# The first stage of a one-core Fourier-mixing and SwiGLU kernel, re-ordered: loads, PSUM banks and weight products

## The chip, the cores and the metric

The kernel runs on one core of a Trainium2 chip. A core has a matrix engine (TensorE, PE in the profile), three engines for elementwise work (VectorE is DVE, ScalarE is ACT, GpSimd is POOL), and SyncE (SP), which here only issues DMAs. Each engine works through a queue of its own, in order; engines wait for each other by semaphores. ScalarE and GpSimd issue DMAs too, between their computing instructions. The metric is the time of one execution on the device in microseconds, as the median of several.

## The reference

```python
X = np.fft.fft(x, axis=1)          # x: 8 x 3008 x 256, float32
X = np.fft.fft(X, axis=2).real     # 8 x 3008 x 256
t = X.reshape(24064, 256)
g = t @ w_gate                     # 256 x 1536
v = t @ w_val                      # 256 x 1536
out = (g / (1 + exp(-g)) * v) @ w_out   # 1536 x 256
```

## The kernel before, in words

**Mixing.** Of each batch's 3008 rows the kernel computes the transform for 1504, as two parts P (even in the feature index) and Q (odd); sums and differences of the two give a row and its mirror. The feature transform is folded into the weights: `Wp` and `Wq` are the weights multiplied by a cosine and a sine table (`CD`, `SDt`), and `Wm` is `Wq` times -2, with which PSUM goes from a row to its mirror by accumulation.

**The row transform of batch 0** is the first stage (lines 257 to 664). The 3008 rows are four quarters of 752. Rows that share a cosine are added before any product: a row that counts up from a quarter's start (a "rise") and one that counts down from its end (a "fall"). 128 such pairs per quarter are the long set (tile `XA`: entries 0 to 3 are the rises, 4 to 7 the falls), 60 per quarter the short set (`XC0`, two quarters above each other in the partitions). Falls come from memory in groups of four rows in another order, so the rises are brought into the same order by a product with a permutation matrix (`place`, line 433, with `putA` or `putC`): its result lies in PSUM. `cross` or `cross_halves` (446, 449) adds the falls with the features turned round; `half_fold` (459) and `fold_d` (495) add or subtract the lower and the upper half of the features, which gives the even sums and the odd sums; `ends` (454) handles feature 0. `half_cast` (499) makes bfloat16 of them. Then `half_folded` (484, long set) and `folded_c` (490, short set) multiply the sums with cosine and sine tables (`Tab`) into two pairs of PSUM banks, `acc[0]` for the even and `acc[1]` for the odd sums; `row0` (619) adds row 0's contribution; `even_copy` (515) and `first_puts` (641) write the tiles `Pt` and `Qt`, the operands of the main stage. `first_w` (502) makes the first 512 columns of `Wp` and `Wq` from the raw weights that `load_w` (389) loads through GpSimd's queue, and `double` (511) makes `Wm` of them on GpSimd.

Everything in this stage stands in the order in which it is written, on each engine's queue. At its start SyncE issues all rises of the long set as one DMA (line 261), two falls, the rises of the short set (267) and its falls (270); ScalarE issues two falls of the long set (264); GpSimd issues the middle rows of the short set (404). TensorE meanwhile multiplies the all-zero matrix `sel` by itself 48 times (306). The tables' angles are computed on GpSimd (`turns`, 362) and VectorE (`angles`, 366), the sines on ScalarE. PSUM's eight banks are eight slots for the whole kernel: three named g, three v, two o; the first stage takes its banks from them.

**The main stage** (from line 666) runs over 24 tiles of up to 512 columns and 12 blocks of 128 hidden features each: products for gate and value (line 1015), silu on ScalarE, products on VectorE and GpSimd, and the output product with `w_out` (1279). The rest of the weights (products at 1501) and the transforms of batches 1 to 7 (1453) are put between. Its order on each engine is planned by a small scheduler in the kernel (`Sched`, from estimated durations and due times), and the plan starts from fixed offsets, so it does not depend on how long the first stage takes. The tiles of the main stage lie in the memory that the first stage's scratch (`tp`, `tq`) leaves.

The order around the change, after the tables:

```python
    psA = place(XA, putA, 4, ((psG, "g"), (psV, "v")))
    warm(8)
    for a in range(2):
        cross(FA[:, a], XA, psA, a)
```

Of the kernel before, what the change touches and what calls it, by code (L numbers as in the profile page):

```python
# [19 lines left out]
def kernel(  # L20
# [67 lines left out]
    Tab = const.tile([P, 2, 2, 2, NTAB], BF16, name="Tab")  # L88
    halfpi = const.tile([P, 1], F32, name="halfpi")
# [31 lines left out]

    def up_block(b, j, n):
        return rows_at(b, 2 * j - 1, [[2 * D, n], [R * D, 4], [1, 2 * D]])
# [121 lines left out]
    Ec0 = tp.tile([P, 2, 2, 1], F32, name="Ec0")  # L245
# [15 lines left out]
    q.dma_start(out=XA3[:, 0:4, :], in_=up_block(0, 1, P))  # L261
# [24 lines left out]
    nc.gpsimd.iota(putA, pattern=[[-LA, NA], [1, LA]], base=JA - 1, **iota)  # L286
# [6 lines left out]
    for a in range(2):  # L293
        fall_c(1, a, q)
        fall_c(0, a, q)
# [7 lines left out]
    for i in range(4):  # L303
        ps = psO.tile([P, T], F32, name="o")
        for j in range(12):
            nc.tensor.matmul(ps[:, 0:P], sel, sel, start=True, stop=True)
# [7 lines left out]
    mm_ = col("mm", 4)  # L314
# [28 lines left out]
    def turn_signs():  # L343
        n_ = col("n_", 4, I32)
# [10 lines left out]
    vts(putA, putA, scalar1=pcol, scalar2=None, op0=Alu.is_equal)  # L355
# [51 lines left out]
    nc.gpsimd.memset(sel[0:1, :], 1.0)  # L407
# [22 lines left out]
    weigh_ce()  # L430
    opposite(0)

    def place(X, put, n, pools):
        pss = []
        for a in range(n):
            pool, nm = pools[a % len(pools)]
            ps = pool.tile([P, 2, D], F32, name=nm)
            nc.tensor.matmul(ps.rearrange("p q d -> p (q d)"), put, X[:, a].rearrange("p q d -> p (q d)"),
                             start=True, stop=True)
            pss.append(ps)  # L440
        return pss

    def falling(X, pss, a):
        return (X[:, 7 - a] if len(pss) == 4 else X[:, 2 + a])[:, ::-1]

    def cross(to, X, pss, a):
        vtt(to[:, :, 1:D], pss[a][:, :, 1:D], falling(X, pss, a)[:, :, D - 1:0:-1], op=Alu.add)

    def cross_halves(to, X, pss, a):
        down = falling(X, pss, a)  # L450
        vtt(to, pss[a][:, :, 1:P + 1], down[:, :, D - 1:P - 1:-1], op=Alu.add)
        vtt(pss[a][:, :, P:D], pss[a][:, :, P:D], down[:, :, P:0:-1], op=Alu.add)

    def ends(to, X, pss, a):
        vtt(to, pss[a][:, :, 0:1], falling(X, pss, a)[:, :, 0:1], op=Alu.add)
# [3 lines left out]
    def half_fold(eo, to, low, pss, a):  # L459
        vtt(to, low[:, :, ::-1], pss[a][:, :, P:D], op=SUMS[eo])  # L460
# [8 lines left out]
    def warm(n):  # L469
        ps = psO.tile([P, T], F32, name="o")  # L470
        for i in range(n):
            nc.tensor.matmul(ps[:, 0:P], sel, sel, start=True, stop=True)

    def start_acc(eo):
        for q, (pool, nm) in enumerate(((psV, "v"), (psG, "g"))):
            acc[eo][q] = pool.tile([P, T], F32, name=nm)
# [7 lines left out]
    def half_folded(eo, a0, first):  # L484
        for q in range(2):
# [33 lines left out]

    psG.at = psV.at = 2  # L520
    psA = place(XA, putA, 4, ((psG, "g"), (psV, "v")))
    warm(8)
    for a in range(2):
        cross(FA[:, a], XA, psA, a)
    for a in range(2):
        ends(Eh[:, a], XA, psA, a)
    row_signs()
# [4 lines left out]
    for a in range(2, 4):  # L532
        cross_halves(FA[:, a, :, 1:P + 1], XA, psA, a)
    for a in range(2, 4):
        half_fold(0, EOA[0][1][:, a - 2], FA[:, a, :, 1:P + 1], psA, a)
    for a in range(2, 4):
        ends(Eh[:, a], XA, psA, a)
    start_acc(0)
    start_acc(1)
    psC = place(XC0, putC, 2, ((psO, "o"),))  # L540
    half_cast(0, 0)
    for a in range(2, 4):
        nc.scalar.copy(FA[:, a, :, P + 1:D], psA[a][:, :, P + 1:D])
    half_cast(0, 2)
    nc.scalar.activation(Z0.rearrange("p q k d -> p (q k d)"), zero.to_broadcast([P, 6 * P]), AF.Copy)
    opposite(1)
# [16 lines left out]
    for fn in early[5:]:  # L563
        fn()
    load_w(1, (0,))
    fold_d(1, 2)
# [3 lines left out]
    ptt(EOb[:, 1, 0:2], EOA[1][0], EOA[1][1], op=Alu.add)  # L570
    half_folded(0, 0, True)
# [9 lines left out]
    for a in range(2):  # L581
        half_fold(1, EB[:, 1, a], FC[:, a], psC, a)
# [78 lines left out]
    for c in copies[2:4]:  # L661
        c()
# [1102 lines left out]
```

## Time and profile before

| | us |
|---|---|
| median of 3 runs (lowest to highest) | 597.71 (597.52 to 597.75) |
| the profiled execution | 597.77 |
| its span, from the first instruction to the last | 596.0 |
| TensorE busy | 590.9 (99%) |
| VectorE, ScalarE, GpSimd busy | 568.6, 553.6, 533.5 (95%, 93%, 90%) |
| first product of the main stage starts | 18.20 |

A timeline row gives the start in us, the duration, the engine, the line of the kernel, the operation, the tiles (out<-in) with their shape, and how many instructions are merged in it; in brackets stands how long the engine was idle before it, and what released it. A row of a table of stretches gives for each engine the busy time and, in parentheses, the number of instructions, then the granted TensorE clock, the share of time in which the DMA engines were busy and the GB/s they moved. A queue row gives packets, MB, and share of the DMA engines. A row of waits gives who waited for whom, the total in us, how often, and the longest. In the DMA rows q1 is SyncE's queue, q10 ScalarE's, q0 GpSimd's. Busy TensorE time counts overlapping matmuls; TensorE is the engine that has no free time in this kernel.

### The profile page before, as it was taken

To read this page: it belongs to the slowest core of one execution; us is meant where nothing else is said; L and a number is where in the kernel's file an instruction comes from. 1 tells how busy PE (TensorE), PEld (TensorE's weight loads), DVE (VectorE), ACT (ScalarE), POOL (GpSimd) and SP (SyncE) were. 2 spreads that over 40 slices of the span, in tenths; PEclk is the share of its full clock that TensorE was granted. 3 is DMA by queue.
4 is the path that set the end of the run, shared out by engine and by line. 5 is a ranking of instruction groups with operands and counts; after the bars stand their busy time and mean duration, and the time that the engine had idled before them with its cause. 6 is when DMAs were issued, how large, how long until landed. Compare 5 with 4: busy or idle time off the path is not lost.

```text
span 596.0 us, 12394 instructions
## 1 busy us (share of the span) xinstructions
PE 590.9 (99%) x4014; PEld 390.6 (66%) x4014; DVE 568.6 (95%) x1062; ACT 553.6 (93%) x1071; POOL 533.5 (90%) x491
## 2 busy tenths in 40 slices
PE   9999999999999999999999999999999999999997
PEld 6456676666666666666666666666666666666686
DVE  9989999999999999999999999999999999999993
ACT  8768989999998899899999999999999999999995
POOL 9979999999999999999899998999889868687782
PEclk9999999999999999999999999999999999999999
DMA  9976772756244255285125122054121103202212
GB/s 251 161 222 229 185 235 71 194 165 222 82 149 126 73 139 137 68 273 159 54 82 168 37 64 63 19 152 143 46 63 37 47 19 88 67 28 63 60 54 81
DMA packets 61070, 68.17 MB, mean 114 GB/s; under 512 B 6744, under 2 KB 48668, under 8 KB 61006
## 3 DMA queue, kind: packets, MB, share of 16 engines
q1 hardware_dynamic: 57422, 64.44, 36.1%
q0 software_dynamic: 3216, 2.36, 2.9%
q8 instruction: 31, 0.51, 0.4%
q10 hardware_dynamic: 368, 0.59, 0.3%
q14 instruction: 33, 0.27, 0.2%
HBM read 40.21 MB, written 35.43 MB: 127 GB/s over the span
## 4 chain that ended last, share of the span: by engine, by line
PE 96%; DVE 0%; ACT 0%; issue 0%
PE o L1279 41%; PE g L1015 27%; PE v L1015 21%; PE g L1453 2%; PE o L1453 2%; PE v L1279 1%; PE o L1501 1%; PE g L622 0%; PE o L622 0%; PE g L1279 0%; PE o L1582 0%; PE g L1650 0%; DVE Wp L508 0%; ACT es L1289 0%; DVE Qt L646 0%
## 5 line engine op out<-in xcount | busy, mean ns | idle before, releaser
L1226 POOL TENSOR_TENSOR hm<-sv 128x1024 bf16<-128x1024 f32 (+2 forms) x137 | 254.7, 1862 | 32.3 <-ACT sv L1202 12.9
L1218 DVE SCALAR_TENSOR_TENSOR sv<-es,v 128x512 f32<-128x512 f32 (+2 forms) x262 | 174.0, 670 | 5.9 <-PE v L1015 4.3
L1279 PE MATMUL o<-Wo,hm 128*128 128x256 bf16 (+1 forms) x1128 | 163.7, 273 | 0.0
L1279 PE MATMUL o<-Wo,hp 128*128 128x256 bf16 (+1 forms) x1104 | 161.1, 272 | 0.0
L1229 DVE TENSOR_TENSOR hp<-sp,v 128x512 bf16<-128x512 f32 (+2 forms) x228 | 151.6, 671 | 1.9 <-PE v L1015 1.1
L1279 PEld LDWEIGHTS <-hm 128*128 128x128 bf16 (+2 forms) x1140 | 111.9, 98 | 58.0 <-issue 0.6
L1279 PEld LDWEIGHTS <-hp 128*128 128x128 bf16 (+2 forms) x1140 | 111.8, 98 | 55.3 <-issue 0.3
L1202 ACT ACTIVATE sv<-g 128x512 f32<-128x512 f32 (+2 forms) x181 | 119.0, 675 | 3.6 <-PE g L1015 3.1
L1127 ACT ACTIVATE sp<-g 128x512 f32<-128x512 f32 (+2 forms) x181 | 112.1, 621 | 5.9 <-PE g L1015 4.0
L1015 PE MATMUL g<-Pt,Wp 128*128 128x512 bf16 (+2 forms) x288 | 107.5, 374 | 0.0
L1015 PE MATMUL v<-Pt,Wp 128*128 128x512 bf16 (+2 forms) x288 | 106.2, 375 | 0.2 <-DVE Wp L508 0.2
L1015 PE MATMUL g<-Qt,Wq 128*128 128x512 bf16 (+2 forms) x288 | 105.4, 375 | 0.1
L1088 ACT ACTIVATE v<-bc,w 128x512 f32<-128x512 bf16 (+2 forms) x139 | 100.3, 726 | 1.9 <-DVE sv L1218 1.0
L1152 DVE SCALAR_TENSOR_TENSOR es<-bc,w,v 128x512 f32<-128x512 bf16 (+2 forms) x135 | 97.9, 732 | 2.1
L1150 ACT ACTIVATE es<-v 128x512 f32<-128x512 f32 (+2 forms) x139 | 86.0, 621 | 3.2 <-PE v L1015 1.6
L1015 PEld LDWEIGHTS <-Wp 128*128 128x128 bf16 x576 | 56.3, 98 | 26.0 <-DVE Wp L508 1.0
L1015 PE MATMUL g<-Qt,Wm 128*128 128x512 bf16 (+2 forms) x195 | 73.1, 376 | 0.0
L1131 DVE SCALAR_TENSOR_TENSOR sg<-bc,w,g 128x512 f32<-128x512 bf16 (+2 forms) x93 | 67.3, 724 | 1.6 <-PE g L1015 1.4
L1235 POOL TENSOR_TENSOR hp<-sp,pp 128x512 bf16<-128x512 f32 (+1 forms) x46 | 57.2, 1245 | 8.0 <-ACT pp L1232 7.8
L1202 ACT ACTIVATE sv<-sg 128x512 f32<-128x512 f32 (+2 forms) x93 | 63.6, 695 | 0.5 <-DVE sg L1195 0.5
L1195 DVE SCALAR_TENSOR_TENSOR sg<-sg,g 128x512 f32<-128x512 f32 (+2 forms) x93 | 61.6, 663 | 0.2
L1015 PEld LDWEIGHTS <-Wq 128*128 128x128 bf16 x437 | 42.7, 98 | 27.5 <-issue 0.4
(218 smaller groups left out, 788.7 us busy)
## 6 DMA issues: line engine op xcount, KB each, us to landing
out_dram<-ev SPq DMA_DIRECT2D x96, 128.0 KB
XA<-in_x_dram SPq DMA_DIRECT2D x30, 256.0 KB
tA<-in_x_dram SPq DMA_DIRECT2D x28, 256.0 KB
XA<-tA SPq DMA_DIRECT2D x14, 512.0 KB
XC<-in_x_dram SPq DMA_DIRECT2D x28, 120.0 KB
tC<-in_x_dram SPq DMA_DIRECT2D x28, 120.0 KB
XC<-tC SPq DMA_DIRECT2D x6, 480.0 KB
bc<-br SPq DMA_DIRECT2D x19, 128.0 KB
```

The source lines that it names most:

```text
L1015: nc.tensor.matmul(ps[:, :n], Wt[:, gv, fs], src[:, :n], start=start, stop=stop, skip_group_check=True)
L1088: nc.scalar.activation(T_[kv][:, :w], bc[t][:, :w], AF.Copy, scale=w0[:, 1, f:f + 1])
L1127: nc.scalar.activation(sp_to()[:, :w], T_[kg][:, :w], AF.Silu)
L1131: nc.vector.scalar_tensor_tensor(T_[keg][:, :w], bc[t][:, :w], w0[:, 0, f:f + 1], T_[kg][:, :w], op0=Alu.mult, op1=Alu.add)
L1150: nc.scalar.activation(T_[kes][:, :w], T_[kv][:, :w], AF.Copy, scale=2.0 if on_pool(u) > 1 else 1.0)
L1152: nc.vector.scalar_tensor_tensor(T_[kes][:, :w], bc[t][:, :w], w0[:, 1, f:f + 1], T_[kv][:, :w], op0=Alu.mult, op1=Alu.add)
L1195: nc.vector.scalar_tensor_tensor(T_[kgm][:, :w], T_[keg][:, :w], 2.0, T_[kg][:, :w], op0=Alu.mult, op1=Alu.subtract)
L1202: nc.scalar.activation(sv()[:, f % 2, w - 1::-1, 1], T_[kgm if by_dve else kg][:, :w], AF.Silu)
L1218: nc.vector.scalar_tensor_tensor(sv()[:, f % 2, w - 1::-1, 0], T_[kes][:, :w], 2.0, T_[kv][:, :w], op0=Alu.mult, op1=Alu.subtract)
L1226: nc.gpsimd.tensor_tensor(hts_(t)[1][:, f - 1:f + 1, :w], sv()[:, :, :w, 1], sv()[:, :, :w, 0], op=Alu.mult)
L1229: nc.vector.tensor_tensor(hts_(t)[0][:, f, :wp], T_[ksp][:, :wp], T_[kv][:, :wp], op=Alu.mult)
L1279: nc.tensor.matmul(st["ps"][:n, j, :], hts[t][minus][:, f, c:c + n], Wo[:, f, :], start=(f == 0), stop=(f == nF - 1))
```

## The change

Only the first stage is changed, and where PSUM banks come from in it.

- **Loads.** The rises of the long set are two DMAs of 512 KB (`rises_a(0)`, `rises_a(2)`) instead of one of 1 MB. ScalarE issues falls 3 and 2 (before: 3 and 1). SyncE issues rises 0 and 1, rises 2 and 3, fall 1, the short set's rises, fall 0 (before: rises, fall 2, fall 0, short set's rises). The middle rows of the short set are loaded by SyncE between the short set's falls, not by GpSimd.
- **Warm-up.** 33 products before the first placement instead of 48, and 5 after the second and 5 after the fourth placement instead of 8 after the fourth.
- **Banks.** The stage has PSUM pools of its own (`first_ctx`: one of two banks, six of one), closed at its end; then psG, psV and psO are made. The third and fourth set lie side by side in the pool of two banks, so `half_fold` and `ends` take both in one instruction.
- **Order on VectorE.** The comparison for `putA` goes to GpSimd (with its iota, between the two pairs of turns). The crossing of the fourth set comes after the ends of the first two. The turn signs come ahead of the first `first_puts`. All four weight copies come between `first_puts` of the even and of the odd sums.
- **Order on TensorE.** The first gate weights (`first_w(0, ...)`) come right after the first half of the even sums, the value weights (`first_w(1, ...)`) before the odd sums; row 0 is done for one half of the odd sums at a time, and the copy of that half (`even_copy(1)`) stands between.
- **Order on ScalarE.** `opposite(0)` before `weigh_ce`, `opposite(1)` before the clearing of `Z0`.
- **Order on GpSimd.** `fold_d(1, 2)` and the sum into `EOb` come before the load of the second gate weights (`load_w(1, (0,))`), the heads after it; the row signs and the setting of `sel`'s first row come at the end of the stage, ahead of `double`.
- **Scratch.** `mm`, `Ec0` and `n_` lie in a new constant tile `mEc` and in `turn_sign`, not in scratch.

```diff
-    psG = Slots("psG", 3, space=bass.MemoryType.PSUM)
-    psV = Slots("psV", 3, space=bass.MemoryType.PSUM)
-    psO = Slots("psO", 2, space=bass.MemoryType.PSUM)
+    first_ctx = ExitStack()
+    banks = [first_ctx.enter_context(tc.tile_pool(name=f"bank{i}", bufs=1, space=bass.MemoryType.PSUM)) for i in range(7)]
...
+    def rises_a(a):
+        q.dma_start(out=XA3[:, a:a + 2, :], in_=rows_at(0, R * a + 1, [[2 * D, P], [R * D, 2], [1, 2 * D]]))
...
+    rises_a(0)
     nc.scalar.activation(w0[:, 0, 0:1], zero, AF.Silu)
     fall_a(3, nc.scalar)
-    fall_a(2, q)
-    fall_a(1, nc.scalar)
+    rises_a(2)
+    fall_a(2, nc.scalar)
+    fall_a(1, q)
+    rises_c(q)
     fall_a(0, q)
-    rises_c(q)
...
+    fall_c(1, 0, q)
+    q.dma_start(out=XC0[NCR:64 + NCR + 1:64, 2:4, 0], in_=rows_at(0, 0, [[2 * R * D, 2], [R * D, 2], [1, D]]))
+    fall_c(0, 0, q)
+    for hi in (1, 0):
+        fall_c(hi, 1, q)
...
+    warm(33)
...
     turns(ti[0], kf, 0)
+    nc.gpsimd.iota(putA, pattern=[[-LA, NA], [1, LA]], base=JA - 1, **iota)
+    pts(putA, putA, scalar1=pcol, scalar2=1.0, op0=Alu.is_equal, op1=Alu.mult)
     turns(ti[1], kf, 1)
     more_iotas()
-    nc.gpsimd.dma_start(out=XC0[NCR:64 + NCR + 1:64, 2:4, 0],
-                        in_=rows_at(0, 0, [[2 * R * D, 2], [R * D, 2], [1, D]]))
...
-    psA = place(XA, putA, 4, ((psG, "g"), (psV, "v")))
-    warm(8)
...
-    row_signs()
+    place(b0, XA, putA, 0)
+    place(b1, XA, putA, 1)
+    warm(5)
+    place(b23[:, 0], XA, putA, 2)
+    place(b23[:, 1], XA, putA, 3)
+    warm(5)
+    for a, ps in enumerate((ps0, ps1)):
+        cross(FA[:, a], ps, down01[:, a])
     load_w(0, (0,))
     fold_d(0, 0)
     load_w(0, (1,))
     fold_d(1, 0)
...
+    cross_halves(FA[:, 2, :, 1:P + 1], ps23[:, 0], down23[:, 0])
+    for a, ps in enumerate((ps0, ps1)):
+        ends(Eh[:, a], ps, down01[:, a])
+    cross_halves(FA[:, 3, :, 1:P + 1], ps23[:, 1], down23[:, 1])
+    half_fold(0, EOA[0][1], FA[:, 2:4, :, 1:P + 1], ps23)
+    ends(Eh[:, 2:4], ps23, down23)
...
+    fold_d(1, 2)
+    ptt(EOb[:, 1, 0:2], EOA[1][0], EOA[1][1], op=Alu.add)
     load_w(1, (0,))
-    fold_d(1, 2)
+    half_folded(0, 0, True)
...
+    turn_signs()
     hd = tp.tile([P, 2, 2, 1], F32, name="hd")
...
-    half_folded(0, 0, True)
+    first_ws = two_banks(0)
+    copies = [first_w(0, k, 1, first_ws[:, k]) for k in range(2)]
     half_folded(0, 2, False)
...
     od0 = even_copy(0)
...
+    copies += [first_w(1, k, k, one_bank(3 + k)) for k in range(2)]
+    start_acc(1, 5, 6)
     for a in range(2):
         folded_c(1, a, True)
-    half_folded(1, 0, False)
...
     nc.gpsimd.iota(kfO, pattern=[[4, GH]], base=1, **iota)
+    row_signs()
+    nc.gpsimd.memset(sel[0:1, :], 1.0)
...
     first_puts(0, od0, (0, 1))
+    for c in copies:
+        c()
     for i in range(2):
+        half_folded(1, 0, False, (i,))
         row0(0, i, acc[1][i])
-    copies[0]()
-    copies[1]()
-    turn_signs()
-    od1 = even_copy(1)
-    copies += [first_w(1, k, k, psO.tile([P, T], F32, name="o")) for k in range(2)]
-    first_puts(1, od1, (0,))
-    for c in copies[2:4]:
-        c()
-    first_puts(1, od1, (1,))
+        if i == 0:
+            od1 = even_copy(1)
+    first_puts(1, od1, (0, 1))
     tmp_ctx.close()
+    first_ctx.close()
+
+    psG = Slots("psG", 3, space=bass.MemoryType.PSUM)
```

More of the change, by code (lines that the diff above doesn't have):

```diff
@@ L301, in more_iotas, with warm @@
             nc.gpsimd.iota(putC[:, pm - NCR:pm], pattern=[[-2 * LC, NC_], [2, LC]], base=2 * (NCR - LC) + hi, **iota)
[L303 to L306, printed above, removed]
+    def warm(n):
+        for i in range(n):
+            nc.tensor.matmul(idle[:, 0, 0:P], sel, sel, start=True, stop=True)
+    warm(33)
     small = {}
@@ L467, with start_acc, of_sets @@
     acc = [[None, None], [None, None]]
[L469 to L476, printed above, removed]
+    def start_acc(eo, *at):
+        acc[eo] = [one_bank(i) for i in at]
+    def of_sets(bank):
+        return bank.rearrange("p a (q d) -> p a q d", q=2) if len(bank.shape) == 3 else bank.rearrange("p (q d) -> p q d", q=2)
     def set_cols(ps, tab, a):
```

111 lines of the change are left out of this document (48 added, 63 removed).

## The prediction

> **What bounds the kernel now.** I read the page first, then who waited for whom on TensorE, then the instructions of the first 24 us in order of time, engine by engine, then the DMA of the same stretch.
>
> ```profile
> span 596.0 us, 12394 instructions
> ```
>
> ```profile
> PE v L1015 <- DVE Wp L508: 0.2, 1, 0.2
> ```
>
> Beside its start, this is the only wait of TensorE (PE) in the run: after 19.5 us it never stands still, and the order on each engine in the main stage is the same in both kernels. So what the first stage gains or loses on TensorE by about 22 us is what the kernel gains or loses.
>
> ```profile
> 1.04 5.30 PE L306 MATMUL o<-sel 128*128 128x128 bf16 x48 [1.04 <-DVE sel L258]
> 6.13 1.36 PE L438 MATMUL g<-XA,putA 128*128 128x512 f32 x2
> ...
> 9.91 0.61 PE L472 MATMUL o<-sel 128*128 128x128 bf16 x8
> 10.36 1.94 PE L438 MATMUL o<-XC,putC 128*128 128x512 f32 x4
> 12.13 0.48 PE L488 MATMUL v<-Tab,EOb 128*128 128x377 bf16 x2
> ...
> 18.20 0.57 PE L1015 MATMUL g<-Pt,Wp 128*128 128x480 bf16 x2
> 18.90 0.36 PE L1015 MATMUL g<-Qt,Wq 128*128 128x480 bf16 x1
> 19.50 0.38 PE L1015 MATMUL v<-Pt,Wp 128*128 128x480 bf16 x1 [0.24 <-DVE Wp L508]
> ```
>
> TensorE runs on without a gap: 48 warm-up products to 6.13, four placements of the long set, 8 warm-ups, two placements of the short set, and from 12.13 to 18.20 (6.07 us) the sums, the first weights and row 0. Then it is held up at 18.90 by the odd tile and at 19.50 by a weight copy. The change touches just these: the warm-up count, the load before the first placement, the weight copy.
>
> **The change part by part.**
>
> *Rises in halves, 33 warm-ups.* In the stretches from 0, GB/s (the last column) times time is what the DMA has moved; below stand the queues up to 5.5 us, and SP's last two loads of the first stage:
>
> ```profile
> 0.00:4.00 4.00, 2.96 (x28) 2.97 (x29) 3.12 (x27) 3.24 (x6) 3.22 (x13) 1.00 0.46 136
> 0.00:9.00 9.00, 7.96 (x54) 6.50 (x55) 8.05 (x37) 7.92 (x13) 7.90 (x23) 1.00 0.79 279
> ```
>
> ```profile
> q1 hardware_dynamic: 524, 1.05, 58.5%
> q10 hardware_dynamic: 38, 0.08, 3.6%
> ```
>
> ```profile
> 5.97 1.81 SPq L270 DMA_DIRECT2D XC<-in_x_dram  x2
> ```
>
> The rises (1.05 MB) were through by 5.5 us, and the SP load that waits for their landing went out at 5.97: landing is 0.47 us behind the last byte. A half is 0.52 MB; 136 GB/s x 4.0 us = 0.54 MB, so the first half lands at about 4.0 + 0.47 = 4.5. The warm-ups cost (6.13 - 1.04) / 48 = 106 ns each; 33 end at 4.55. The first placement starts at 4.6 instead of 6.13.
>
> The eight later warm-ups took (10.36 - 9.91) / 8 = 56 ns, half as much: the clock doubled in between, and the first placement (1.36 us, against half of the short set's 1.94) shows that it did so around 6.1 to 7.5. Starting at 4.6, the first placement (at full speed (12.13 - 10.36) / 2 = 0.88) therefore costs 0.88 x 106 / 56 = 1.67, the second about 1.0, the other two 0.88 each, with 0.28 for 5 warm-ups ahead of them and behind: 9.6. The short set's rises now queue behind 1.05 MB and three falls of 0.26: through at 2.36 MB, 8.5 us by 279 GB/s, landed by 9.2 even if 0.2 late. Their placements run from 9.6 to 11.4, not 10.36 to 12.13. TensorE has gained 0.75 us there.
>
> *The last fall now queues behind the short set's rises*, at the mark of 2.62 MB instead of 2.10. 279 x 9 = 2.51 MB, so 9.4 at that rate, landed at 9.85 at the earliest; some 0.8 later, 10.6, if the first weight load (0.26 MB), which is issued 0.9 us earlier than before, goes through the engines ahead of it. I take 10.1, nearer the early end, as that load is issued after it. Who needs the fall is the crossing of the fourth set:
>
> ```profile
> 10.11 0.43 DVE L451 TENSOR_TENSOR FA<-v,XA 128x256 f32<-128x256 f32 x1
> ...
> 11.71 0.41 DVE L451 TENSOR_TENSOR FC<-o,XC 128x256 f32<-128x256 f32 x1
> ```
>
> ```profile
> 12.08 0.38 ACT L543 COPY FA<-v 128x254 f32<-128x254 f32 x1
> ```
>
> The crossing ran at 10.11. VectorE (DVE), relieved of the comparison for putA, comes to it about 0.4 us earlier and then stands until 10.1. Two sets folded at a time is the same elements in two instructions fewer (together below 0.15 us). So VectorE reaches the short set at 11.7 (11.71), and ScalarE (ACT) ends its copies of the upper halves at 12.08 + 0.38 = 12.46, as before. The gain of the placements stops here.
>
> *Weights ahead of the odd sums.* VectorE's end of the stage was:
>
> ```profile
> 15.73 1.20 DVE L646 TENSOR_TENSOR Pt<-g,od 128x188 bf16<-128x188 f32 x5 [0.64 <-ACT od L517]
> ...
> 18.07 0.77 DVE L646 TENSOR_TENSOR Qt<-g,od 128x188 bf16<-128x188 f32 x3
> 18.77 0.68 DVE L508 CAST Wp<-o 128x512 bf16<-128x512 f32 x1
> ```
>
> TensorE begins the sums at 11.4. After the first four products (0.65) come the first weights, into the two banks that ScalarE's copies free at 12.46: a wait of 0.5. So the main stage starts at 11.4 + 6.07 + 0.5 = 18.0 (18.20). VectorE fills its 0.64 us of idle time with the turn signs, moved ahead, and takes the weight copy in front of the odd tile: 18.07 - 0.64 + 0.68 = 18.11, no change for the odd tile, and 18.90 stays. But the value product of 19.50 then follows at once, at 19.15: 0.35 us gained.
>
> *What is pushed behind on GpSimd (POOL)*, which issues DMAs and computes in one queue:
>
> ```profile
> 7.25 0.19 POOL L407 MEMSET sel<- 1x128 bf16 x1
> 7.53 0.47 POOL L357 TENSOR_SCALAR sgo<-pc 128x1 f32<-128x1 f32 x1
> 8.12 0.26 POOL L358 TENSOR_SCALAR sgo<-sgo,sgn 128x1 f32<-128x1 f32 x1
> 8.32 0.82 POOL L394 DMA_DIRECT2D W<-in_moe_w_gate_dram  x1
> ...
> 12.03 0.73 POOL L394 DMA_DIRECT2D XA<-in_moe_w_gate_dram  x1
> 12.78 1.10 POOL L497 TENSOR_TENSOR Fc<-FA 128x512 f32<-128x512 f32 x1
> ...
> 18.89 1.35 POOL L512 TENSOR_SCALAR Wm<-Wq,m 128x512 bf16<-128x512 bf16 x2
> ```
>
> ```profile
> 21.79 0.37 PE L1015 MATMUL v<-Qt,Wm 128*128 128x480 bf16 x1
> ```
>
> The odd fold (12.78) needs ScalarE's copies and starts at 12.46 + 0.1 = 12.57. From it to the doubling of the mirrored weights Wm (18.89) were 6.11 us. Into this stretch come the weight load from ahead of the fold (12.78 - 12.03 = 0.75), the row signs (8.32 - 7.53 = 0.79) and sel's memset (0.19): 1.73. The doubling starts at 12.57 + 6.11 + 1.73 = 20.41 and its second half ends 1.35 later, at 21.76. TensorE used that half at 21.79 and, 0.35 us earlier, would want it at 21.44. It gets it at 21.9, a semaphore's 0.1 later: the 0.35 us are lost in this wait, and 0.1 with them. POOL then is 1.5 us late on work that TensorE asks for much later.
>
> *The middle rows' DMA from POOL to SP; putA's iota and comparison between POOL's two pairs of turns.* POOL drops an issue and gains a comparison, and has putC by 7.5, wanted at 9.6. SP has one issue more among its short loads; they ended at 5.97 + 1.81 = 7.78, and their data stand behind 2.6 MB anyway. Nothing.
>
> *opposite(1) ahead of clearing Z0* on ScalarE: Z0 is ready one copy later, below 1 us; SP's next loads wait for it, and for those the first fold of batch 1:
>
> ```profile
> 39.17 2.35 POOL L181 TENSOR_TENSOR SDf<-XC 128x1020 f32<-128x1020 f32 x1 [1.95 <-DVE hp L1053]
> ```
>
> POOL stood 1.95 us before that fold with nothing else due: no cost; without that cover, up to 1 us on POOL. Scratch moved: no instruction.
>
> **Sum.** +0.1 us. The profiled execution took 597.77 us (the span of 596.0 and 1.8 around it), 0.06 above the median of 597.71. Forecast 597.8; of its own 597.5 to 598.4, as the last fall lands from 9.85 (-0.25) to 10.6 (+0.5).
>
> **The rivals.**
>
> *The gain stays.* If POOL is at the doubling 0.4 us earlier than I add up, TensorE keeps its 0.35: 597.4. For it: the fall may land early, and two rows of one form on POOL differ by up to 0.1 us. Against it: 1.73 us of moved work. More than 0.2% (1.2 us, about what can be told from no change here) would need the doubling at 19.1, which the rows exclude.
>
> *The clock does not rise in time (slower).* Before, TensorE was busy without a break from 1.04 until the clock rose. Now it may stand between 4.55 and the first half's landing. If that keeps half speed through all four placements they end at 4.6 + 4 x 1.67 + 0.5 = 11.8, and the fourth set is crossed at 11.8 instead of 10.1, +1.7; if the clock rises during the third, +1.1. The chains of VectorE and POOL shift by it: 598.9 to 599.5. [...]
> The Trainium skill, "TensorE: Matmul & The Clock Gate", Part 1 (the HAM clock gate), says that the clock is released after a busy window of about 3.4 us which runs free of the kernel's start; the 106 and 56 ns above agree with its cold and warm spacing. By that rule any gap before the release is a risk.
> The Trainium skill, "DMA: Bandwidth & Descriptors", Queues, rings and completion order, says that an engine serves its queues in turn, packet by packet. By it the fall on ScalarE's queue would mix with the first half, which would land about 0.65 us later and open such a gap. The queue rows speak against it: by 5.5 us queue 10, ScalarE's, had moved 0.08 MB.
>
> *A weight load comes late (slower).* The load of 12.03 is now issued behind the odd fold and sum, at 12.57 + 1.10 + 1.26 = 14.9. The sum's row, the landing of the four weight loads into XA, and the first product with one of them:
>
> ```profile
> 14.42 1.26 POOL L570 TENSOR_TENSOR EOb<-Fc 128x512 bf16<-128x512 f32 x1
> ```
>
> ```profile
> DMA to landing us min/median/max: 5.0/5.5/7.8
> ```
>
> ```profile
> 20.52 0.59 PE L1501 MATMUL o<-XA,CD 128*128 128x512 bf16 x2
> ```
>
> At 5.5 us to landing it is there at 20.4; that product stood at 20.52 and is wanted at 20.2, a wait inside the one above. At the longest landing of these loads, 7.8, it is 22.7 and TensorE loses 2.2 against before: 599.9. It decides from 5.7 us on. Against it: the load of 12.03 landed in a queue of first-stage loads that is gone by 15.
>
> *The halves do nothing.* If the first half lands no earlier than the whole did (5.97), placements start at 6.0, the short set's at 10.0, and all limits behind stay: 597.8 again, with the clock's risk.
>
> **How the numbers follow.** POOL's wait, +0.1: 0.52. The gain stays: 0.18. Halves do nothing, same time: 0.06. Clock: 0.12. Late weight load, or another loss of its size in the main stage: 0.10. Far faster by something unseen: 0.02. Faster by over 0.2%: 0.05, with part of the second case; within: 0.77; slower: 0.18, part of the clock's lying at the edge. The range of 8 in 10 takes in the first two cases and the lower half of the clock's: 597.1 to 599.1.
>
> **What would show it.** First placement at 4.6 and longer than 1.36; the short set's at 9.6; the fourth set crossed at 10.1 after a wait of VectorE for a DMA; main stage begun at 18.0, its first value product right behind the odd tile at 19.15; the doubling at 20.4, and a wait of TensorE for Wm from POOL of about 0.4 us near 21.5, the only new one. Wrong if the doubling starts by 20.0, if placements after the second take over 1.2 us, or if TensorE waits for a weight load.

## The result, and the profile after

The changed kernel takes 599.62 us (median of 7 runs, 598.79 to 600.42) against 597.71 (7 runs, 597.40 to 597.92): a ratio of 1.0032, 95% interval 1.0020 to 1.0043. It is slower by 1.9 us, where no change was forecast (597.8, with 8 chances in 10 between 597.1 and 599.1). Its runs also lie further apart: 1.6 us from lowest to highest, 0.5 before. (That 0.5 is of seven runs. Of the 121 runs of the kernel before that were made beside all the experiments, 11 lie above 598.5, up to 599.66; no profile shows why.) The profiled run has the lowest time of the seven (598.79, span 597.0), so it shows only a part of the loss, 1.0 us of span.

The waits of TensorE in the changed kernel behind its start (who waited for whom, total, how often, longest):

```profile
PE b L505 <- ACT FA L549: 0.7, 1, 0.7
PE o L1513 <- DMA XA<-in_moe_w_gate_dram: 0.5, 1, 0.5
PE g L1027 <- DVE Qt L656: 0.4, 1, 0.4
PE b L493 <- DVE EOf L463: 0.3, 1, 0.3
```

None of them is the one forecast, for `Wm`. The first and the third were in the sum; the fourth was not; the second is the rival of the late weight load. In order of time, on TensorE:

```profile
4.85 2.24 PE L445 MATMUL b<-XA,putA 128*128 128x512 f32 x4
...
9.59 1.96 PE L445 MATMUL b<-XC,putC 128*128 128x512 f32 x4
11.39 0.81 PE L488 MATMUL b<-Tab,EOb 128*128 128x377 bf16 x4
12.85 0.59 PE L505 MATMUL b<-W,CD 128*128 128x512 bf16 x2 [0.66 <-ACT FA L549]
...
18.68 0.58 PE L1027 MATMUL g<-Pt,Wp 128*128 128x480 bf16 x2
19.70 0.36 PE L1027 MATMUL g<-Qt,Wq 128*128 128x480 bf16 x1 [0.44 <-DVE Qt L656]
...
21.58 0.60 PE L1513 MATMUL o<-XA,CD 128*128 128x512 bf16 x2 [0.51 <-DMA XA<-in_moe_w_gate_dram]
...
22.86 0.37 PE L1027 MATMUL v<-Qt,Wm 128*128 128x480 bf16 x1
```

The first half of the stage gains what was forecast: the sums begin at 11.39, not 12.13. By the main stage it is gone (18.68 against 18.20), and at the product that stood at 21.79 the kernel is 1.07 us late. On VectorE and on GpSimd:

```profile
10.37 0.43 DVE L452 TENSOR_TENSOR FA<-b,XA 128x256 f32<-128x256 f32 x1
...
11.98 0.41 DVE L452 TENSOR_TENSOR FC<-b,XC 128x256 f32<-128x256 f32 x1
...
13.76 0.42 DVE L452 TENSOR_TENSOR FC<-b,XC 128x256 f32<-128x256 f32 x1 [0.44 <-DMA XC<-in_x_dram]
...
18.86 1.20 DVE L656 TENSOR_TENSOR Qt<-b,od 128x188 bf16<-128x188 f32 x5 [0.70 <-PE b L638]
```

```profile
12.88 1.09 POOL L497 TENSOR_TENSOR Fc<-FA 128x512 f32<-128x512 f32 x1 [0.95 <-DVE b L453]
14.04 1.27 POOL L572 TENSOR_TENSOR EOb<-Fc 128x512 bf16<-128x512 f32 x1
15.25 0.74 POOL L407 DMA_DIRECT2D XA<-in_moe_w_gate_dram  x1
...
20.72 1.36 POOL L512 TENSOR_SCALAR Wm<-Wq,m 128x512 bf16<-128x512 bf16 x2
```

The four weight loads into `XA`, from issue to landing:

```profile
DMA to landing us min/median/max: 6.2/6.8/9.2
```

(5.0/5.5/7.8 before). The gate load goes out 3.2 us later than before (15.25 against 12.03), and these loads now take 1.2 to 1.4 us longer. The gate load itself took 5.0 us before and 6.3 now, so that it lands 4.5 us later (21.5 against 17.1).

### The profile page after: what moved, and what is told of

Its sections match the earlier page's. It is cut to its first block, busy times and chain, and to the rows that moved or that the text cites. A ratio compares the mean times of both kernels' runs of the same rounds, so it can differ in the third digit from the quotient of the medians.

```text
span 597.0 us, 12369 instructions
## 1 busy us (share of the span) xinstructions
PE 590.4 (99%) x4001; PEld 388.9 (65%) x4001; DVE 568.6 (95%) x1059; ACT 553.4 (93%) x1071; POOL 534.3 (89%) x491
## 4 chain that ended last, share of the span: by engine, by line
PE 97%; DMA 1%; POOL 1%; DVE 1%; issue 0%; ACT 0%; DVEq 0%; POOLq 0%
PE o L1291 41%; PE g L1027 27%; PE v L1027 21%; PE g L1465 2%; PE o L1465 2%; DMA XA<-in_moe_w_gate_dram 1%; PE b L445 1%; PE v L1291 1%; PE o L1513 1%; PE o L632 0%; PE g L632 0%; PE g L1291 0%; DVE b L453 0%; POOL EOb L572 0%; POOL t L377 0%
```

## The experiments

Times are given as the ratio of the means to the kernel before, run beside it on the same chip, with the 95% interval; 0.001 is 0.6 us. The changed kernel stands at 1.0032. The first load of gate weights into `XA` is called the gate load; the second sequence is batch 1, the loads of which SyncE issues behind those of the first stage.

### One order or one transfer undone

**gate_load_early**: the second chunk of the gate weights is loaded where it was loaded before.

```diff
+    load_w(1, (0,))
     fold_d(1, 2)
     ptt(EOb[:, 1, 0:2], EOA[1][0], EOA[1][1], op=Alu.add)
-    load_w(1, (0,))
```

> The changed kernel, but the second chunk of the gate weights is issued where it was before the change: ahead of the odd fold on POOL, not behind it and the sum EOb. Theory 1 (the late gate load is the loss): the issue goes from 15.25 to about 12 us, the data land at 17 to 18, the wait of 0.51 us of PE in L1513 for the gate weights goes, and the median falls by 0.5 us or more below the changed kernel's 599.6, with a smaller scatter. Theory 2 (the short set's falls arrive late, so the even and odd folds of the short set and the tiles Pt and Qt come late): the wait is only exchanged for another one, PE's first tile starts at 18.7 as in the changed kernel, and the median falls by less than 0.2. Theory 3 (the moved row signs and the memset hold up the doubled weights): nothing changes that is beyond 0.2.

Measured: 1.0018 (1.0009 to 1.0028), 598.13 to 599.98. The load goes out at 11.84, the wait for it is gone, and in this kernel's timeline the product of 22.86 stands at

```profile
21.88 0.37 PE L1027 MATMUL v<-Qt,Wm 128*128 128x480 bf16 x1
...
23.66 0.60 PE L1513 MATMUL o<-XA,CD 128*128 128x512 bf16 x2 [0.40 <-ACT sg L1083]
```

that is 0.09 behind the kernel before, as the sum of the prediction had it; another 0.40 comes right behind. By the ratios some 0.8 us of the 1.9 go. The scatter stays (1.9 us): this is not the whole cause. (The two intervals overlap; the run before_gate_late below settles the mechanism.)

**middle_on_pool**: the middle rows' load goes back to GpSimd. **both_back**: both edits.

```diff
     fall_c(1, 0, q)
-    q.dma_start(out=XC0[NCR:64 + NCR + 1:64, 2:4, 0], in_=rows_at(0, 0, [[2 * R * D, 2], [R * D, 2], [1, D]]))
     fall_c(0, 0, q)
...
     more_iotas()
+    nc.gpsimd.dma_start(out=XC0[NCR:64 + NCR + 1:64, 2:4, 0], in_=rows_at(0, 0, [[2 * R * D, 2], [R * D, 2], [1, D]]))
```

> The changed kernel, but the middle rows of the short set are issued by POOL behind its last tables, as before the change, so that SP has one issue less between its short falls. Theory 2 (SP's issue stands behind a semaphore of an earlier load, so that the last two short falls land at 12.97 and 13.63 in place of 11.69 and 12.19): the short set's second fold on DVE no longer waits 0.44 us for its data, Qt comes 0.4 to 0.7 earlier, and the median falls by 0.4 to 0.7 us below the changed kernel. Theory 1 (late gate load): the first tiles come earlier, but PE then waits that much longer for the gate weights, and the median falls by less than 0.2.

> The changed kernel with both: the gate load ahead of the odd fold and the middle rows on POOL. If theories 1 and 2 each hold a part, the gains add up: 1.0 us or more below the changed kernel in the profile, near the kernel before. If only one of them is the cause, this run equals the better of the two single ones within 0.2.

Measured: 1.0036 (1.0024 to 1.0048) and 1.0017 (1.0008 to 1.0026). The wait of VectorE for the short set's falls is not there, and in middle_on_pool the main stage starts at 18.44; the time does not fall. (Two further profiles of the changed kernel itself, below, lack that wait too, so the edit need not have removed it.) Both edits together are no better than the gate load alone. Theory 2, the late falls of the short set, falls as a cause of the loss. The profile of middle_on_pool (span 598.8) shows something else, a wait of TensorE in the main stage, near 62 us, taken up below.

**rises_whole**: the rises are one DMA again.

```diff
-        q.dma_start(out=XA3[:, a:a + 2, :], in_=rows_at(0, R * a + 1, [[2 * D, P], [R * D, 2], [1, 2 * D]]))
+        q.dma_start(out=XA3[:, a:a + 4, :], in_=rows_at(0, R * a + 1, [[2 * D, P], [R * D, 4], [1, 2 * D]]))
...
-    rises_a(2)
```

> The changed kernel, but the long set's rises are one DMA again, first on SP, and the falls keep the changed order and queues. The prediction's step 1 says that this costs the 0.75 us by which the short set is placed earlier, and nothing at the end, because the last fall sets the fourth crossing: within 0.2 of the changed kernel. Theory 2 says that one DMA less on the hardware queues shifts which load each later issue waits for: the last two short falls leave earlier, and the median falls by 0.3 to 0.7. Theory 4 (what scatters is the time of the clock's release, which hangs on when PE begins its unbroken work): a later first placement changes the scatter of the runs, not the waits.

Measured: 1.0066 (1.0050 to 1.0082), 600.16 to 603.26. Within the stage the forecast holds: TensorE waits 1.61 us for the rises, and the main stage starts at 18.84, only 0.16 later than with halves. But the wait for the gate weights grows to 0.72 (the load goes out at 15.92), and a wait of 0.68 for ScalarE follows at 29.6. So the halves are worth 2 us here by the ratios, and most of what the profile shows of it lies behind the stage; what the longer runs add to it no profile shows. Theory 4, that the clock's rise makes the scatter, finds no support: in the three profiles of the changed kernel the first two placements take 2.24, 2.51 and 1.98 us, as the clock rises later or earlier in them, but the sums begin at 11.39, 11.38 and 11.16, 0.23 us apart, and the spans lie 2.1 apart.

**zeros_early**: ScalarE clears `Z0` before its copies of `FA`. **zeros_and_gate_early**: this and the gate load.

```diff
     half_cast(0, 0)
+    nc.scalar.activation(Z0.rearrange("p q k d -> p (q k d)"), zero.to_broadcast([P, 6 * P]), AF.Copy)
     for a in range(2, 4):
         nc.scalar.copy(FA[:, a, :, P + 1:D], ps23[:, a - 2, :, P + 1:D])
     half_cast(0, 2)
     opposite(1)
-    nc.scalar.activation(Z0.rearrange("p q k d -> p (q k d)"), zero.to_broadcast([P, 6 * P]), AF.Copy)
```

> The changed kernel, but ACT writes the zeros Z0 before the copies of FA, in the 1.27 us in which it waits, and not after the opposite tables. SP's first zero fill of XC, which waits for Z0, then leaves at 12 to 13 us in place of 14.80 (13.74 in the kernel before), and every load of the second sequence behind it on SP with it. Theory 5 (the second sequence's loads are late: POOL's fold of XC at 40.3 instead of 39.2, and when it comes much after 40.3, as at 41.54 and 41.93 in two runs above, POOL's products come late and ACT and PE wait for them): the fold of XC begins before 39.5, and the median falls from 599.6 to 598.6 to 599.0, with a scatter of under 1 us; the profile's waits in the first 25 us stay (0.51 for the gate weights, 0.44 for Qt). Theory 1 (only the gate load): the median stays within 0.3 of 599.6. Against both: the earlier loads compete with the short set's falls and the first weights, and the first tile comes later than 18.7.

> The changed kernel with the zeros Z0 early on ACT and the gate load ahead of the odd fold on POOL. Theories 1 and 5 together: no wait for the gate weights, the fold of XC before 39.5, and what is left of the loss is the later first tiles (0.3 to 0.5 us): a median of 598.0 to 598.4 with the small scatter of the kernel before (0.5 us). If the median is still above 598.8 though both waits are gone, a third cause is missing. If it falls below 597.7, the change itself was a gain that these two orders hid.

Measured: 1.0054 (1.0033 to 1.0076), 598.75 to 603.40, and 1.0017 (1.0008 to 1.0025). The fold of `XC` does come early (38.8 and 38.6 us) and nobody waits for it, but in zeros_early TensorE gains a wait of 0.8 us for the first value weights, which landed in 6.1 us and not 4.7, and one of 1.3 us for an output buffer near 260 us. SyncE's zero fill and its loads start at 11.6 there and may have run into the weights; but zeros_and_gate_early starts them as early and has no such wait, so this is not shown. This expectation failed.

**gate_early_fall_first**: the gate load early, and the last fall ahead of the short set's rises.

```diff
-    rises_c(q)
     fall_a(0, q)
+    rises_c(q)
```

> The changed kernel with the gate load ahead of the odd fold and the last fall on SP ahead of the short set's rises. The prediction held that the gain of the earlier placements stops at the last fall, which lands at 10.1 to 10.5 behind the short set's rises. If so, the fourth crossing on DVE comes 0.3 or more earlier and the median falls by 0.2 to 0.3 below that of the run with the gate load alone (ratio to before 1.0018). If DVE itself sets the fourth crossing, or the short set's rises are as urgent, the median is the same within 0.2 or higher.

Measured: 1.0017 (1.0008 to 1.0026), the same as without this edit (1.0018). The place of the last fall does not set the end.

### The gate load in the kernel before

**before_gate_late** moves that one load in the kernel before, and nothing else.

```diff
-    load_w(1, (0,))
     fold_d(1, 2)
...
     ptt(EOb[:, 1, 0:2], EOA[1][0], EOA[1][1], op=Alu.add)
+    load_w(1, (0,))
```

> The kernel before, with one thing changed: the second chunk of the gate weights is issued behind the odd fold, the sum hd and the sum EOb on POOL (about 14.9 us, not 12.03). Theory 1: the data land at 20.2 to 21.5 us, PE's product for it, which began at 20.52, waits up to 1.0 us, and the median rises by 0.3 to 1.0 us. If the load has slack beyond that: within 0.2 of the kernel before.

Measured: 1.0025 (1.0015 to 1.0035), +1.5 us, and the runs lie close together (598.78 to 599.36). Its only new wait of size (one of 0.27 us for GpSimd, at 17.0, is made up by 19.4):

```profile
PE o L1501 <- DMA XA<-in_moe_w_gate_dram: 1.4, 1, 1.4
```

```profile
DMA to landing us min/median/max: 6.6/8.0/10.3
```

This is shown, then: the new place of this load costs 1.4 us by itself. In the changed kernel a part of it overlaps with TensorE's own lateness: TensorE comes to the product at 21.07, and at 20.78 and 20.55 in the two profiles that follow (20.52 before), and waits 0.51, 0.91 and 0.84, so that the product starts between 21.39 and 21.69 in all three.

### Where the runs differ

**after_look2**, **after_look3**: the changed kernel, profiled twice more.

> The changed kernel itself, profiled once more, since its profile on record came from the fastest of seven runs (598.79 against a median of 599.62). If the missing 0.8 us lies in the first stage, the wait for the gate weights is longer than 0.51 (up to 1.4, as in the kernel before with the late gate load). If it lies with the second sequence's loads, POOL's fold of XC begins after 41 us and ACT or PE wait for POOL's product near 60 us.

> The changed kernel a third time, for the same question: the waits of PE that stand here or in the second look and not in the profile on record are where the runs differ.

They took 600.59 (span 598.8) and 598.51 (596.7). The longest waits of the first:

```profile
PE v L1027 <- ACT es L1162: 1.0, 1, 1.0
PE o L1513 <- DMA XA<-in_moe_w_gate_dram: 0.9, 1, 0.9
PE b L505 <- ACT FA L549: 0.7, 1, 0.7
PE g L1027 <- DVE Qt L656: 0.4, 1, 0.4
PE v L1027 <- ACT v L1100: 0.4, 1, 0.4
```

At 22 us the two stand at +1.18 and +0.88, close to each other. The first loses 0.39 more near 62 us and 0.97 near 263 us; the second has neither wait. So the first 22 us cost about 1 us in each of the three profiles, and late waits add to it in one.

**The wait near 62 us.** In middle_on_pool ScalarE's, TensorE's and GpSimd's rows for it are

```profile
54.02 0.64 ACT L1301 COPY ev<-o 128x256 f32<-128x256 f32 x2 [1.23 <-PE o L1291]
...
61.48 0.64 ACT L1214 ACTIVATE sv<-g 128x512 f32<-128x512 f32 x1 [1.22 <-POOL hm L1238]
...
62.74 0.38 PE L1027 MATMUL v<-Pt,Wp 128*128 128x512 bf16 x1 [1.16 <-ACT v L1100]
...
41.93 2.35 POOL L190 TENSOR_TENSOR SDf<-XC 128x1020 f32<-128x1020 f32 x1 [3.60 <-DVE Qt L1482]
```

GpSimd's fold of the second sequence's short set (`SDf<-XC`) starts when its loads have landed; GpSimd's product `hm` near 60 us comes behind it, ScalarE waits for that and TensorE for ScalarE. The copy at 54.02, which TensorE feeds, serves as a mark for TensorE's own progress; in the kernel before it is

```profile
52.92 0.64 ACT L1289 COPY ev<-o 128x256 f32<-128x256 f32 x2 [1.23 <-PE o L1279]
```

From fold to mark:

| kernel | fold starts | mark | mark minus fold | TensorE waits near 62 us |
|---|---|---|---|---|
| before | 39.17 | 52.92 | 13.75 | 0 |
| changed | 40.32 | 54.20 | 13.88 | 0 |
| after_look3 | 40.56 | 54.06 | 13.50 | 0 |
| after_look2 | 41.59 | 54.44 | 12.85 | 0.39 |
| gate_early_fall_first | 41.61 | 54.34 | 12.73 | 0.53 |
| gate_early_13_more | 41.25 | 53.36 | 12.11 | 1.15 |
| middle_on_pool | 41.93 | 54.02 | 12.09 | 1.16 |
| before_loads_late | 42.09 | 52.45 | 10.36 | 2.88 |

The wait is 13.25 less the distance, to 0.01 us in all five rows that wait; both_back, at 13.28, and gate_load_early, at 13.38, have none. The kernel before has 0.50 us to spare, and in these rows whatever made the fold later than that relative to TensorE was paid in full.

**before_loads_late** tries this in the kernel before; **before_clear_late** was the first attempt.

```diff
     copies[1]()
+    nc.scalar.activation(zeros, zero.to_broadcast([P, D]), AF.Copy)
+    clear_c(1)
...
```

The zeros are written a second time, and the whole block of SyncE's zero fills and loads stands behind that.

> The kernel before, with one thing changed: SP's zero fill of XC and the second sequence's loads behind it wait for a second writing of the zeros by ACT at about 16.6 us (no new tile, so that no buffer is reused behind it). Theory 5: POOL's fold of XC moves from 39.2 to 41.5 to 42.5, as in the run with the middle rows on POOL (41.93), POOL's products near 60 us come late, ACT and PE wait 1 to 2 us there, and the median rises by 1 to 3 us. If these loads have slack: within 0.3 of the kernel before.

> The kernel before, with one thing changed: SP's zero fill of XC and the second sequence's loads behind it wait for a small write of ACT at about 16.6 us (of 128x256 zeros, ahead of the second sums' copy) and not for Z0 at 13.7. Nothing of the first stage waits for them. Theory 5: POOL's fold of XC moves from 39.17 to 41.5 to 42.5, POOL's products and then ACT and PE come late as in the middle rows' run, and the median rises by 1.0 to 3.0 us, with more scatter than the kernel before has. If the loads have slack: within 0.3 of the kernel before.

before_loads_late: 1.0066 (1.0053 to 1.0078). Its one wait:

```profile
PE v L1016 <- ACT v L1089: 2.9, 1, 2.9
```

The mechanism is shown: nothing that the first stage waits for changed, the fold went from 39.17 to 42.09, and the wait came at the place and in the size that the other rows of the table give. (The span grew by 4.3 us, more than the wait; the last section takes this up.) before_clear_late (1.0166) wrote the zeros into a new tile of the scratch instead, the memory of which the main stage uses again. ScalarE waited there long before the fold:

```profile
ACT sg L1051 <- DMA XC<-in_x_dram: 9.9, 1, 9.9
```

This is most likely the wait for that memory. The run disturbed something else than it was to test, and says nothing on theory 5, the late loads of the second sequence.

### The loads in another order

SyncE's loads from memory into `tC` go ahead of the eight direct loads of `XC`, in four kernels.

```diff
     clear_c(1)
+    early = reorder("C", 1, q) + reorder("A", 1, q)
+    for fn in early[:4]:
+        fn()
     for k in range(2):
         for a in range(4):
             down_c1(a, k, q)
```

**before_turned_first**: 

> The kernel before, with SP's order changed behind the first zero fill: the four loads into the scratch tC go ahead of the eight direct loads of XC, so that the two loads from tC into XC, on which POOL's fold waits last, no longer wait for them. In the kernel before that fold begins at 39.2 us, and the runs so far say that PE waits for what it comes later than 39.9 on PE's own clock. Theory 5: the fold begins 2 us or more earlier, and since nothing waited for it, the median stays within 0.2 of the kernel before.

**before_turned_first_loads_late**: 

> The same order, and the whole chain of second sequence's loads held back to 16.9 us as in the run before_loads_late, whose PE was 0.7 us ahead of the kernel before until 53 us and then waited 2.9 us for POOL's fold at 42.1. Theory 5: the fold begins before 39.9, the wait of 2.9 is gone, and the 0.7 us stay: 597.0 of the 597.7. If the 0.7 us were not the loads' competition with the weights, the median is that of the kernel before.

Measured: 0.9998 (0.9989 to 1.0007) and 1.0000 (0.9991 to 1.0009). The fold begins at 38.69 and 38.63; with the loads held back as in before_loads_late its wait of 2.9 us is gone, and 4 us come back. The 0.7 us of gain that was hoped for (0.47 at the mark) is not there: before_13_fewer, with these loads untouched, shows the same early mark (52.47), so holding back the loads is not needed for it; most likely it is variation from run to run.

**gate_early_turned_first**: 

> The changed kernel with the gate load ahead of the odd fold and SP's order with the tC loads first. Theory 5: the fold of XC begins 2 us earlier, no run waits for POOL near 62 us, and the scatter of the run gate_load_early (598.13 to 599.98) shrinks to its lower end: a median of 598.1 to 598.4, that is 0.4 to 0.7 above the kernel before. If the scatter stays, the later wait near 262 us (for an output buffer) is a cause of its own and not a consequence.

**gate_early_turned_first_loads_late**: 

> The same, and the chain of second sequence's loads held back behind the first weights' copies (17.9 us). What is still open is whether the changed first stage itself is a loss or only its transfers. If only its transfers: the first tiles come 0.5 to 1.0 us earlier, no wait for the gate weights, and the median is at or below that of before_turned_first_loads_late (597.0). If the new order of the first stage itself loses (PE stands at 12 to 13 us for ACT's copies), it stays 0.3 or more above that run.

Measured: 1.0026 (1.0016 to 1.0036) and 1.0020 (1.0011 to 1.0028). Nobody waits near 62 us any more. But in the first TensorE now waits 0.79 us for value weights at 24 us and 0.41 for gate weights at 26 us, and the second, whose profiled run is 0.3 us of span above the kernel before, still has a median 1.3 us above it. The order is no remedy for the changed kernel.

### The length of TensorE's program

All profiles of the changed kernel show four transfers of `Fc` into `St` near 248 us that keep SyncE longer than before, and the waits near 260 us stand behind them. Theory 6 is that the place of TensorE's code makes both: the changed kernel has 13 matmuls fewer ahead of the main stage.

**before_13_fewer** (the kernel before) and **gate_early_13_more** (gate_load_early) change only how many matmuls TensorE's program has ahead of the main stage.

```diff
-        for j in range(12):
-            nc.tensor.matmul(ps[:, 0:P], sel, sel, start=True, stop=True)
+        for n in [2] * (3 + i // 3) + [1] * (6 - 2 * (i // 3)):
+            nc.tensor.matmul(ps[:, 0:n * P].rearrange("p (n d) -> p n d", n=n), sel, sel.unsqueeze(1).to_broadcast([P, n, P]),
+                             start=True, stop=True)
```

```diff
+    for i in range(13):
+        nc.tensor.matmul(spare[0:1, 0:1], sel[:, 0:1], sel[:, 0:1], start=True, stop=True)
     first_ws = two_banks(0)
```

> The kernel before with the same warm-up time out of 13 matmuls fewer (13 of the 48 are 256 columns wide, so that 35 take the time of 48; the zeros are multiplied as before). Nothing else changes but that PE's program is 26 instructions shorter ahead of the main stage, as it is in the changed kernel. Theory 6: PE's code is fetched in blocks of 16 KB; in the kernel before a block is fetched at 245.7 us, in all runs of the changed kernel at 248.8 to 250.0, just when SP issues the four stack transfers of Fc into St, which then take 3.0 to 3.7 us in place of 2.47; the output transfers behind them come late, and in some runs ACT waits 0.3 to 1.4 for an output buffer near 260 us, and PE with it. If so, these four take 3.0 us or more here, and the median rises by 0.3 to 1.0 with runs up to 599. If the place of the blocks does not matter: within 0.2 of the kernel before and 2.47 us for the four.

> The changed kernel with the gate load ahead of the odd fold, and 13 matmuls of one column more, in the time in which PE waits behind the first half sums, so that PE's program ahead of the main stage has the length of the kernel before. Theory 6: the four transfers of Fc into St take 2.47 us again, no run waits for an output buffer near 260 us, and the median falls from 1.0018 of the kernel before to 1.0006 to 1.0012, with less scatter. If the place of the blocks does not matter: the median and scatter of gate_load_early.

The four transfers on SyncE's queue, in the kernel before, the changed one, before_13_fewer and gate_early_13_more:

```profile
246.99 2.47 SPq L1422 DMA_DIRECT2D St<-Fc  x4
```

```profile
248.12 3.24 SPq L1434 DMA_DIRECT2D St<-Fc  x4
```

```profile
246.66 3.12 SPq L1423 DMA_DIRECT2D St<-Fc  x4
```

```profile
248.73 2.46 SPq L1437 DMA_DIRECT2D St<-Fc  x4
```

The four issues follow the count in both directions. The time does not: 0.9993 (0.9984 to 1.0001) and 1.0021 (1.0012 to 1.0030). Theory 6 falls as a cause of the loss.

## Why the prediction was wrong, step by step

- *Halves, warm-ups, placements*: right. First placement 4.85 (4.6), the first two in 2.24 (2.7), the short set's at 9.59 (9.6), the sums at 11.39 (11.4). The clock did not stay low; that rival falls. Even a wait of 1.61 us ahead of the first placement, in rises_whole, left it up: there the first two placements took 1.96 us together.
- *The last fall stops the gain*: the gain does stop about there, by a little more: the fourth crossing at 10.37 (10.1), the short set at 11.98 (11.7). The fall has a small part in it at most: VectorE reaches the crossing without waiting in this profile, waits 0.26 for the fall in after_look3 and 0.17 in gate_load_early, and with the fall put first the time is the same.
- *Main stage at 18.0*: 18.68, and 18.39 and 18.16 in the two further profiles. The wait for ScalarE's copies was 0.66 to 0.8 (0.5), and in the first profile alone the short set's falls landed late, 0.3 on TensorE. That is the step "SP has one issue more among its short loads", which I had costed at nothing: SyncE issued the last three of these from 7.19 on, not from 4.98. *Odd tile unchanged at 18.9*: 19.70, 19.41, 19.18. I moved the weight copy and forgot that the odd puts now wait for TensorE's second half of the odd sums with row 0 (0.70 on VectorE).
- *The doubling at 20.41, TensorE waits for `Wm`*: the doubling came at 20.72, 20.70, 20.60, nearly as summed, and nobody waited for it, because **the same lateness of GpSimd had already struck at the load ahead of it**. This is the step that failed. I wrote that the gate load, issued at 14.9, is there at 20.4 and its wait lies inside the one for `Wm`. It went out at 15.25 and took 6.3 us, to 21.5. The reason that I gave against it, that the queue of first-stage loads is gone by 15, left out what stands there then: SyncE's zero fill from 14.8 and its loads of the second sequence from 15.6 on, and the three weight loads that follow within 3.1 us. That SyncE's loads count shows in the kernels with the old first stage: the value load issued at 15.6 to 15.8 lands in 5.0 to 6.0 us in three of them (before, before_13_fewer, before_turned_first), and in 4.1 and 4.4 where SyncE's loads are held back (before_loads_late, before_turned_first_loads_late). What share of the 6.3 us is theirs was not measured. The rival had the right mechanism, and the landing lay beyond its decision point (5.7 us); a chance of 0.10 was too small, since half of the four loads in the row of before took the 5.5 us with which I reckoned, or longer. Moved alone in the kernel before it costs 1.5 us, about two thirds of its price of 2.2; undone in the changed kernel it gives back 0.8 of the 1.9.
- *The second sequence's fold has 1.95 us of cover*: wrong. That was GpSimd's idle time ahead of the fold, not the slack behind it; the slack is 0.50 us by the table, and one of the three profiled runs of the changed kernel paid for it (0.39).

What stays open is the other 1.1 us of the 1.9, and with it the scatter. With the gate load early all seven kernels tried still stand at 1.0017 to 1.0026, though the lowest time of most is only 0.3 to 0.9 us above the lowest of the kernel before. In their longer profiles TensorE waits for value or gate weights at 23 to 29 us, for GpSimd near 62, or for an output buffer near 260, in changing shares. The median time of the weight loads to landing is 6.8 to 8.5 us in these seven, and 5.5 to 6.6 in the six kernels with the old first stage and the gate load early; which part of the new first stage lengthens them was not isolated. The new PSUM pools and the moved scratch were not tested by themselves either. No version tried beats the kernel before beyond its interval.

## What to carry to other kernels

When work is pushed back on an engine that also issues DMAs, price the loads first and the arithmetic second: a load moved by 3.2 us landed 4.5 us later here, among other transfers, and the wait for it came ahead of the one that was summed. Idle time ahead of an instruction is not slack; slack is measured by delaying the instruction until someone waits, and here a table of delay against wait showed it to 0.01 us. Where runs of one kernel scatter, profile it several times before explaining its median by one profile, all the more if that one has the lowest time.

## What the runs showed of the hardware that was not expected

- **A stall of 2.9 us costs more than itself.** In before_loads_late TensorE stands from 60.0 to 62.9 us. The granted clock (the figure behind the POOL column) is below 1 in the two stretches behind it, and matmuls of 512 columns that took 0.38 us take 0.63 until 66.6:

```profile
60.00:62.00 2.00, 0.01 (x1) 0.00 (x0) 0.36 (x1) 0.36 (x1) 2.00 (x2) 1.00 0.66 213
62.00:66.00 4.00, 3.10 (x13) 1.87 (x13) 2.62 (x5) 3.90 (x8) 4.00 (x4) 0.68 0.51 132
66.00:70.00 4.00, 4.00 (x26) 2.66 (x25) 3.35 (x6) 2.83 (x7) 3.69 (x3) 0.90 0.99 211
```

```profile
63.11 0.38 PE L1016 MATMUL v<-Qt,Wm 128*128 128x512 bf16 x1
...
64.07 0.63 PE L1016 MATMUL g<-Pt,Wp 128*128 128x512 bf16 x1
```

That is 4 x (1 - 0.68) + 4 x (1 - 0.90) = 1.7 us of clock, which with the wait of 2.88 comes to 4.6; less the 0.47 by which the kernel was ahead at the mark this leaves 4.1 of the 4.3 us of span. A wait of 1.2 us near 62 did no such thing: the clock in middle_on_pool is 1.000. In before_clear_late a stall of 8.4 us brought the clock to 0.52 over the 10 us from 25 to 35. The Trainium skill, "TensorE: Matmul & The Clock Gate", Why this matters for your kernels, warns of gaps of more than about 3 us between bursts of matmuls; the gap here, 2.88 us, was a little shorter, and the clock fell all the same.

- **The length of TensorE's program changes the time of SyncE's issues.** 26 instructions (13 matmuls and their weight loads) fewer ahead of the main stage changed four DMA issues some 225 us later from 2.47 to 3.12 us, and 26 more brought them from 3.19 (gate_load_early) to 2.46. In the trace a 16 KB instruction packet, which I take for TensorE's code as it moves with these matmuls, starts at 245.7 us in the kernel before, ahead of the four, and among them, between 247.7 and 250.0, where they take long; in gate_early_13_more it is at 247.4, ahead of them again. All 20 traces agree: 2.46 to 2.48 us in the seven where the packet starts ahead of the four, 2.98 to 3.71 in the thirteen where it starts among them. The Trainium skill, "Runtime: NRT & Kernel Launch", Instruction fetch mechanics, says that engines refill their instructions in 16 KB blocks through a DMA queue and calls the cost mostly hidden; here too it was hidden from the end-to-end time. That the packet itself delays the issues fits, but was not separated from other effects of the code's length.
